# Storing each 512-token output tile with one DMA in place of four, and the last tile in two halves on two queues

## Chip, cores and metric

The kernel runs on one core of one Trainium2 chip. The metric is device time in microseconds (us), the span from the first to the last instruction of an execution. Before the change it took 617.64 us, the median of three runs (613.49 to 619.96). A profiled execution is one run of its own, so its span differs by a few us from the median.

## The reference

Two layers follow one another on `x[8, 3072, 256]` (float32). The first is a frequency mixer along the sequence, the second a gated channel mixer:

```python
def _attn_ref(x, w_r, w_i, b_r, b_i):
    X = np.fft.rfft(x, axis=1)
    Xr, Xi = X.real, X.imag
    Yr = Xr @ w_r - Xi @ w_i + b_r
    Yi = Xr @ w_i + Xi @ w_r + b_i
    # soft threshold of Yr and Yi by 0.01
    return np.fft.irfft(Yr + 1j * Yi, n=x.shape[1], axis=1)

def _moe_ref(x, mu_k, mu_r, w_k, w_v, w_r):
    x_prev = ...                       # x, one token later
    xk = mu_k * x + (1.0 - mu_k) * x_prev
    xr = mu_r * x + (1.0 - mu_r) * x_prev
    k = np.maximum(xk @ w_k, 0.0)      # 256 -> 1024
    v = k * k @ w_v                    # 1024 -> 256
    return 1.0 / (1.0 + np.exp(-(xr @ w_r))) * v
```

## The kernel before

The engines have names in the profiles: PE is the matrix engine, whose results the kernel puts into PSUM (its tile `banks`); DVE and ACT are VectorE and ScalarE. The Fourier transform of 3072 points is split into 96 x 32. Between its two inverse steps the data must change their order, and this goes through device memory: the tile `V` is stored to `Vdr` and read back into `V2`. All these DMAs are issued from the sync queue (`nc.sync`), as the output stores are. Lines are numbered as in the profiles (L465, L476, L523 and so on).

```python
            def store(k):                                   # six of these per batch
                for cj in range(4):
                    nc.sync.dma_start(                                          # L465
                        out=Vdr[b][24 * cj + 4 * u:24 * cj + 4 * u + 4].rearrange("g n d -> n g d"),
                        in_=vt[32 * cj:32 * cj + 32])
                # ... after the sixth of them
            def fetch(k):
                for q in (2, 3, 0, 1):
                    nc.sync.dma_start(out=V2[b, q], in_=Vdr[b][:, 8 * q:8 * q + 8, :])   # L476
# ... cut ...
            # last inverse step: eight such units per batch
            for i in range(4):
                n2 = 16 * half + 4 * i + qd
                for c in range(NCD):
                    nc.tensor.matmul(pv[:, c, :, i, :],                         # L523
                                     V2[b, n2 // 8][:, n2 % 8, 128 * c:128 * c + 128], FI, ...)
```

The last step of the second layer multiplies `v` by the gate and stores 512 tokens. The tile `o` has 128 partitions of 4096 bytes. A tile holds half of each 32 tokens of a third of a batch: partition 32x + s of it has the four neighbouring tokens from number 32s + 16 half + 4x of that third on. So 32 neighbouring partitions go to places 32,768 bytes apart in device memory, and partitions 32 apart go to places 4096 bytes apart:

```python
    def v_unit(t, p):                       # p = 0, 1: two halves of the matmuls
        def issue(ps, h, end):
            # ... 32 matmuls, L653 ...
            if p == 0:
                return
            o, rg = o_pool.tile([128, 4, D], FP32, name="o"), RG[t]      # o_pool has two buffers

            def gated(k):
                nc.vector.tensor_tensor(out=o.rearrange("p q d -> p (q d)"), in0=ps, in1=rg, op=ALU.mult)  # L660
                # ...
            def store(k):
                b, half, hh = t // 6, (t % 6) // 3, t % 3
                rows = out[b].rearrange("(h s z x q) d -> h z x s q d", h=3, s=32, z=2, x=4)
                for xx in range(4):
                    nc.sync.dma_start(out=rows[hh, half, xx], in_=o[32 * xx:32 * xx + 32])   # L669
```

## Time and profile before

| profile of the kernel before | value |
|---|---|
| span | 615.4 us |
| matrix engine busy | 571.8 us, 93% |
| its waits for the V round trip (L523) | 12.6 us |
| its idle time between first and last matmul | 34.5 us |
| last matmul to landing of the last store | 4.85 us |

The matrix engine bounds the kernel. Whatever makes it wait can be expected to cost time. These lines of its page are the clock row (a digit for each fortieth of the span), a group of instructions (busy us, mean ns of one, then the idle time before them and what ended it), and a DMA issue (KB each, median us from issue to landing):

```profile
PEclk9999799999999999989999999999999999999999
...
L523 PE MATMUL banks<-FI,V 96*128 96x96 f16 x512 | 33.5, 216 | 12.9 <-DMA V<-Vdr 12.6
...
out_dram<-o SPq DMA_DIRECT2D x192, 128.0 KB, 2.3
```

The sync queue's own waits (us in total, times, longest):

```profile
SPq L476 <- DMA Vdr<-V: 15.7, 7, 6.2
```

The sync queue waits 15.7 us until V stores have landed, and an output store of 128 KB lands 2.3 us after its issue.

### The profile page before, as it was taken

The numbers are of one execution on the slowest core, as the hardware profiler recorded it, in microseconds if no ns is written. First come the engines' busy times: TensorE is split into PE (matmuls) and PEld (weight loads), VectorE is DVE, ScalarE is ACT, GpSimd is POOL, SyncE is SP. The second block draws the span as 40 slices with busy tenths as digits, with TensorE's granted clock in tenths as the row PEclk, the third lists the DMA queues.
The fourth block names the chain that finished last, engine by engine and source line by source line (L and its number), as shares of the span: only waits on it lengthen the run. The fifth ranks groups of instructions, "written<-read, shape, count | busy, mean of one in ns | idle before, by whom it ended". The sixth has DMA issues, their size and how long they took to land.

```text
span 615.4 us, 12311 instructions
## 1 busy us (share of the span) xinstructions
PE 571.8 (93%) x4823; PEld 431.9 (70%) x4891; DVE 517.6 (84%) x839; ACT 436.0 (71%) x476; POOL 23.3 (4%) x52
## 2 busy tenths in 40 slices
PE   4775899999999999979999999999999999999995
PEld 3764666667777777657776778677776778777664
DVE  6774699878998999959988888979888889989883
ACT  6764596776877677757787768876787777667662
POOL 7001000000000000000000000000000000000000
PEclk9999799999999999989999999999999999999999
DMA  8948237982668755695568946686347833462223
GB/s 150 175 82 181 65 62 166 242 185 55 133 142 236 172 110 132 144 231 118 108 136 200 195 114 129 141 236 147 83 98 189 190 93 87 87 172 65 70 64 78
DMA packets 68686, 84.06 MB, mean 137 GB/s; under 512 B 8978, under 2 KB 53780, under 8 KB 68628
## 3 DMA queue, kind: packets, MB, share of 16 engines
q1 hardware_dynamic: 62916, 69.24, 45.4%
q0 software_dynamic: 5712, 14.03, 14.7%
q8 instruction: 38, 0.62, 0.4%
q14 instruction: 20, 0.16, 0.1%
HBM read 50.07 MB, written 47.19 MB: 158 GB/s over the span
## 4 chain that ended last, share of the span: by engine, by line
PE 79%; DMA 8%; DVE 5%; ACT 5%; issue 2%; SPq 1%; POOL 0%; ACTq 0%; POOLq 0%; DVEq 0%
PE banks L653 25%; PE banks L609 24%; PE banks L426 11%; PE banks L636 6%; DMA V<-Vdr 4%; DMA Vdr<-V 3%; PE banks L523 3%; PE banks L398 3%; PE banks L452 3%; PE banks L280 3%; ACT rl L615 2%; DMA xs<-in_x_dram 1%; DVE Y L442 1%; DVE z L440 1%; DVE V L229 1%
## 5 line engine op out<-in xcount | busy, mean ns | idle before, releaser
L615 ACT ACTIVATE rl<-banks 128x1024 bf16<-128x1024 f32 x192 | 195.4, 1033 | 76.1 <-PE banks L609 75.0
L609 PE MATMUL banks<-xk,wk 128*128 128x512 bf16 x700 | 190.1, 379 | 5.1 <-ACT A L227 0.8
L653 PE MATMUL banks<-wv,k 128*128 128x256 bf16 x1536 | 183.4, 273 | 0.3 <-DVE k L621 0.3
L653 PEld LDWEIGHTS <-k 128*128 128x128 bf16 x1536 | 149.6, 98 | 30.3 <-issue 1.2
L621 DVE TENSOR_TENSOR k<-rl 128x1024 bf16<-128x1024 bf16 x192 | 131.0, 685 | 16.8 <-ACT rl L615 16.1
L609 PEld LDWEIGHTS <-wk 128*128 128x128 bf16 x768 | 73.0, 97 | 59.5 <-issue 3.2
L426 PEld LDWEIGHTS <-XT 128*128 128x128 bf16 x768 | 74.4, 98 | 16.1 <-issue 0.6
L426 PE MATMUL banks<-wr,XT 128*128 128x256 bf16 x384 | 73.5, 273 | 0.2 <-ACT XT L227 0.2
L426 PE MATMUL banks<-wi,XT 128*128 128x256 bf16 x384 | 73.5, 273 | 0.0
L587 DVE SCALAR_TENSOR_TENSOR xk<-diff,muk,YT 128x512 bf16<-128x512 bf16 x96 | 70.0, 745 | 0.5
L587 DVE SCALAR_TENSOR_TENSOR xr<-diff,mur,YT 128x512 bf16<-128x512 bf16 x96 | 68.9, 745 | 0.0
L227 ACT ACTIVATE YT<-banks 128x768 bf16<-128x768 f32 x60 | 46.3, 814 | 30.0 <-PE banks L523 28.1
L660 DVE TENSOR_TENSOR o<-banks,rg 128x1024 f32<-128x1024 f32 x48 | 58.5, 1219 | 6.6 <-PE banks L653 6.6
L227 ACT ACTIVATE z<-banks 128x1024 bf16<-128x1024 f32 x39 | 39.9, 1024 | 23.7 <-PE banks L426 23.7
L227 ACT ACTIVATE XT<-banks 128x1024 bf16<-128x1024 f32 (+2 forms) x45 | 44.4, 989 | 14.3 <-PE banks L398 14.3
L636 PE MATMUL banks<-wrm,xr 128*128 128x256 bf16 x384 | 50.6, 275 | 1.8 <-ACT rl L615 1.7
L641 ACT ACTIVATE rg<-banks 128x1024 bf16<-128x1024 f32 x48 | 49.5, 1031 | 0.9 <-PE banks L636 0.9
L227 ACT ACTIVATE A<-banks 96x1024 bf16<-96x1024 f32 (+1 forms) x43 | 43.4, 1015 | 8.0 <-PE banks L280 6.7
L636 PEld LDWEIGHTS <-xr 128*128 128x128 bf16 x384 | 37.4, 98 | 12.7 <-issue 2.6
L523 PE MATMUL banks<-FI,V 96*128 96x96 f16 x512 | 33.5, 216 | 12.9 <-DMA V<-Vdr 12.6
L227 ACT ACTIVATE V<-banks 128x1024 bf16<-128x1024 f32 x35 | 36.0, 1028 | 13.2 <-PE banks L452 11.1
L523 PEld LDWEIGHTS <-V 96*128 96x128 bf16 x512 | 29.5, 104 | 20.6 <-DMA V<-Vdr 14.7
(98 smaller groups left out, 447.3 us busy)
## 6 DMA issues: line engine op xcount, KB each, us to landing
out_dram<-o SPq DMA_DIRECT2D x192, 128.0 KB, 2.3
xs<-in_x_dram POOLq DMA_DIRECT2D x32, 384.0 KB, 6.2
Vdr<-V SPq DMA_DIRECT2D x192, 64.0 KB, 1.8
V<-Vdr SPq DMA_DIRECT2D x32, 384.0 KB, 6.8
Adr<-A SPq DMA_DIRECT2D x24, 384.0 KB, 5.5
A<-Adr SPq DMA_DIRECT2D x48, 192.0 KB, 5.6
wk<-in_moe_w_k_dram POOLq DMA_DIRECT2D x1, 512.0 KB, 11.6
wv<-in_moe_w_v_dram POOLq DMA_DIRECT2D x1, 512.0 KB, 13.9
```

The costliest lines, as they stand in the source:

```text
L227: nc.scalar.activation(out, in_, AF.Copy, bias=0.0, scale=1.0)
L280: nc.tensor.matmul(ps[:96, 512 * i:512 * i + 512], FT, xt[:, 4 * p + 2 * i:4 * p + 2 * i + 2, :], start=True, stop=True)
L426: nc.tensor.matmul(o, lhs, w[:, c, :], start=(w is wr and c == 0), stop=(w is wi and c == NCD - 1))
L523: nc.tensor.matmul(pv[:, c, :, i, :], V2[b, n2 // 8][:, n2 % 8, 128 * c:128 * c + 128], FI, start=True, stop=True)
L587: nc.vector.scalar_tensor_tensor(out=m[:, c, :], in0=df[:, c, :], scalar=mu[:, c:c + 1], in1=yp[:, c, :], op0=ALU.mult, op1=ALU.add)
L609: nc.tensor.matmul(ps[:, 512 * f:512 * f + 512], wk[:, c, 128 * ff:128 * ff + 128], xk[:, c, :], start=(c == 0), stop=(c == NCD - 1))
L615: nc.scalar.activation(rl, ps, AF.Relu, bias=0.0, scale=1.0)
L621: nc.vector.tensor_tensor(out=k2, in0=rl, in1=rl, op=ALU.mult)
L636: nc.tensor.matmul(ps[:, 256 * q:256 * q + 256], xr[:, c, 128 * q:128 * q + 128], wrm[:, c, :], start=(c == 0), stop=(c == NCD - 1))
L641: nc.scalar.activation(rg, ps, AF.Sigmoid, bias=0.0, scale=1.0)
L653: nc.tensor.matmul(ps[:, 256 * q:256 * q + 256], K2[t][:, ff, 128 * q:128 * q + 128], wv[:, ff, :], start=(ff == 0), stop=(ff == NCF - 1))
L660: nc.vector.tensor_tensor(out=o.rearrange("p q d -> p (q d)"), in0=ps, in1=rg, op=ALU.mult)
```

## The change

Its intent is to save issues on the sync queue (49 output DMAs for 192) and to shorten the end: the last tile is gated in two halves, and the first half is stored from the sync queue while the second is still being computed; the second goes out on the ScalarE queue.

```diff
-            if p == 0:
+            final = t == NT - 1
+            if p == 0 and not final:
                 return
-            o, rg = o_pool.tile([128, 4, D], FP32, name="o"), RG[t]
+            if p == 0 or not final:
+                OT[t] = o_pool.tile([128, 4 * D], FP32, name="o")
+            o, rg = OT[t], RG[t]
+            lo, hi = (512 * p, 512 * p + 512) if final else (0, 1024)
 
             def gated(k):
-                nc.vector.tensor_tensor(out=o.rearrange("p q d -> p (q d)"), in0=ps, in1=rg, op=ALU.mult)
+                nc.vector.tensor_tensor(out=o[:, lo:hi], in0=ps[:, lo:hi], in1=rg[:, lo:hi], op=ALU.mult)
# ... cut ...
             def store(k):
                 b, half, hh = t // 6, (t % 6) // 3, t % 3
-                rows = out[b].rearrange("(h s z x q) d -> h z x s q d", h=3, s=32, z=2, x=4)
-                for xx in range(4):
-                    nc.sync.dma_start(out=rows[hh, half, xx], in_=o[32 * xx:32 * xx + 32])
+                rows = out[b].rearrange("(h s z x q) d -> h z x s (q d)", h=3, s=32, z=2, x=4)[hh, half]
+                (nc.scalar if final and p == 1 else nc.sync).dma_start(out=rows[:, :, lo:hi], in_=o[:, lo:hi])
# ... cut ...
```

The old store writes `[32, 1024]` from 32 partitions, the new one `[4, 32, 1024]` from 128 partitions.

More of the change, by code (lines that the diff above doesn't have):

```diff
@@ L654, in issue @@
                                      wv[:, ff, :], start=(ff == 0), stop=(ff == NCF - 1))
-            if p == 0:
+            final = t == NT - 1
+            if p == 0 and not final:
                 return
-            o, rg = o_pool.tile([128, 4, D], FP32, name="o"), RG[t]
+            if p == 0 or not final:
+                OT[t] = o_pool.tile([128, 4 * D], FP32, name="o")
+            o, rg = OT[t], RG[t]
+            lo, hi = (512 * p, 512 * p + 512) if final else (0, 1024)
             def gated(k):
-                nc.vector.tensor_tensor(out=o.rearrange("p q d -> p (q d)"), in0=ps, in1=rg, op=ALU.mult)
-                e = run_on("dve", k, 1.22)
-                release(h, e)
+                nc.vector.tensor_tensor(out=o[:, lo:hi], in0=ps[:, lo:hi], in1=rg[:, lo:hi], op=ALU.mult)
+                e = run_on("dve", k, 0.7 if final else 1.22)
+                if p == 1:
+                    release(h, e)
                 at(e, store)
@@ L666, in store @@
                 b, half, hh = t // 6, (t % 6) // 3, t % 3
-                rows = out[b].rearrange("(h s z x q) d -> h z x s q d", h=3, s=32, z=2, x=4)
-                for xx in range(4):
-                    nc.sync.dma_start(out=rows[hh, half, xx], in_=o[32 * xx:32 * xx + 32])
+                rows = out[b].rearrange("(h s z x q) d -> h z x s (q d)", h=3, s=32, z=2, x=4)[hh, half]
+                (nc.scalar if final and p == 1 else nc.sync).dma_start(out=rows[:, :, lo:hi], in_=o[:, lo:hi])
+            if p == 0:
+                at(end, gated)
+                return
             done["v_out", t] = end
```

## The prediction

It calls k the number of DMA engines that share one store. For the old store it reads 16 from the starts of packets; 4 for the new one was an assumption of mine, which no trace of the kernel before could show.

> **What bounds the kernel now.** I read the page's busy table and chain first, then the matrix engine's waits, the DMA issues, the sync queue's timeline round the end of one batch, and last the DMA load of single stretches. The page of the kernel before:
>
> ```profile
> span 615.4 us, 12311 instructions
> PE 571.8 (93%) x4823; PEld 431.9 (70%) x4891; DVE 517.6 (84%) x839; ACT 436.0 (71%) x476; POOL 23.3 (4%) x52
> ...
> PE 79%; DMA 8%; DVE 5%; ACT 5%; issue 2%; SPq 1%; POOL 0%; ACTq 0%; POOLq 0%; DVEq 0%
> ```
>
> The matrix engine is busy for 93% of the span and is 79% of the chain that ended last. Its order is fixed when the program is built, so a stall of it is lost. The second owner of the chain is DMA with 8%. The waits of the matrix engine (total us, times, longest) say which DMA:
>
> ```profile
> PE banks L523 <- DMA V<-Vdr: 12.6, 8, 6.3
> PE banks L452 <- DVE Y L442: 5.3, 4, 1.8
> ```
>
> V<-Vdr is a round trip: the tile V is stored to device memory in another order and read back at each batch's end. Output stores appear in no wait of the matrix engine. The sync queue issues all of these; near the end of batch 4 (counted from 0; columns: start, duration, engine, line, what), and the matmuls that need the loads:
>
> ```profile
> 323.55 1.91 SPq L669 DMA_DIRECT2D out_dram<-o  x4
> 325.57 1.84 SPq L465 DMA_DIRECT2D Vdr<-V  x4
> 328.52 0.31 SPq L291 DMA_DIRECT2D Adr<-A  x1
> 329.06 3.03 SPq L476 DMA_DIRECT2D V<-Vdr  x4
> 332.14 2.54 SPq L669 DMA_DIRECT2D out_dram<-o  x4
> 335.92 0.31 SPq L291 DMA_DIRECT2D Adr<-A  x1
> ...
> 338.58 0.51 PE L523 MATMUL banks<-FI,V 96*128 96x96 f16 x8
> ```
>
> An output store is issued just ahead of the batch's last V store, and the second of the V loads, which L523 needs, lands at 337.5, so there is 1.1 us of slack. In batch 3 there is none; its chain of waits holds
>
> ```profile
> 252.06 6.97 DMA Vdr<-V
> ...
> 260.47 8.20 DMA V<-Vdr
> ```
>
> Comparing landing of V loads with the first L523 in every batch, I find slack of about 7 us in batch 1, 0 to 1 in batch 2, 0 in batch 3, 0 to 1 in batch 4, 1.5 in batch 5, 3.5 in batch 6 and 0 in batch 7. Batch 0 has no output stores beside it.
>
> [...] Each old store has 32 rows on both sides[...] its packets start 16 at a time (16 starts from 590.62 to 590.82). The new store is 4 x 32 x 1024 outside and 128 x 1024 inside[...]. No DMA of the kernel before has that shape[...]. [...] The trace's fastest 4096-byte packets take 158 ns, 25.9 GB/s[...].[...]
>
> **The change part by part.**
>
> *Issues.* 192 stores become 47 whole ones and 2 halves, so 143 issues fewer. The median issue takes 0.42 us, so the sync queue is freed of 60 us. It is no bound: 1% of the chain. What that saves on the path is the time by which a V store stands behind the four issues: at 325.57 where the copy of V ended at 325.10, so 0.4 us, and 1.3 us in batch 7 (535.58 against 534.28).
>
> *Engines of a store.* 512 KB is 128 packets of 4096 bytes. On 4 engines each moves 32: 32 x 0.158 = 5.1 us; with 0.8 us from issue to first packet and about 0.5 from last packet to landing, a store lands some 6.4 us after its issue. Now, four issues take 1.7 us and the last lands 2.2 us after its own, so 3.5 us after the first one starts.
>
> *Load of these four engines.* All stores make 48 x 5.1 = 243 us for each. The two large queues take 60.1% of 16 engines' 615 us, 5,920 engine-us; stores are 6,144 packets of about 0.28 us (the tail's median), 1,720; the rest is 4,200, or 262 us per engine. So four engines would be busy for 505 us (82%), the twelve others for 43%. No saturation[...].
>
> *The V store behind an output store.* In batch 4 the store is issued at 323.55 and keeps four engines until 323.55 + 0.8 + 5.1 = 329.45. Their part of the four V stores is 32 packets of 512 bytes at 27 to 44 ns, about 1 us, and 0.8 to landing: 331.2, against 328.75 now. So the loads slip by 2.5 us. The same sum gives about 2 in batches 2, 5 and 7, and I take 3 for batch 3, where an input load shares the engines. Less the slack: 1.5 + 3 + 2.3 + 1 + 0 + 1.8 = 9.6 us of new stalls.
>
> *The A round trip.* Adr<-A at 335.92 stands behind the V loads and the next output store. The stretch is one of full load (columns of the windows view as on the page; DMA share and GB/s are last):
>
> ```profile
> 328.50:345.10 16.60, 16.24 (x144) 12.01 (x144) 13.24 (x24) 12.38 (x14) 0.51 (x1) 1.00 0.88 223
> ```
>
> With 48 packets per engine for the rest instead of 56 and 32 more for the stores on the four, I get 48 x 0.295 + 5.1 = 19.3 us instead of 16.5. The readers of A have 2 to 6 us of slack and the matrix engine is itself late by then, so I count 2 us for the two batches with the least.
>
> *The tail.* Tiles end every 7.8 us there:
>
> ```profile
> 597.60:605.40 7.80, 7.75 (x57) 5.44 (x57) 3.99 (x6) 4.78 (x6) 0.00 (x0) 1.00 0.29 69
> ...
> 609.58 1.22 DVE o L660
> ```
>
> The last gate ends at 610.80, its fourth store lands at 614.34. Halving the gate ends the second half at about 609.58 + 0.65 = 610.2, and the first lies beside the matmuls. But both halves are again on the same four engines, behind the previous tile's store (issued at 605.06, packets from 605.9 to 611.0). The halves add 2 x 2.7 = 5.4 us: 616.4, and 616.9 landed. So the tail gets 2.5 us longer where the intent was about 2 us shorter.
>
> Sum: 9.6 + 2 + 2.5 = 14 us over 617.6, about 632 us.
>
> **The rivals.** *All 16 engines take part after all*[...]. Then only the issue time and the halved tail remain: 1.3 + 0.4 + about 1.8 saved, 614 us, so within 2%. *The four engines are slow but hidden*: [...]the slack of batches 1, 5 and 6 swallows it; the tail alone remains, 620 us. The fact that stores appear in no wait of the matrix engine speaks for it; the zero slack in batches 3 and 7 against it. *The four engines become a bound*: if their packets take 0.25 us or more under mixed load (the median of all 4096-byte packets is 0.252), stores alone take 390 us and the four come near full; every round trip then slips by 5 us or more, and the time goes to 645 us or above.
>
> **Range and chances.** k = 4 I hold for 88% likely. Under it 620 to 648 with the middle at 632, which lies just above the 2% line of 630; without it 612 to 617. Runs of the kernel before spread from 613.5 to 620.0, which blurs the line further. A range of 618 to 648 holds it 8 times in 10. Faster by over 2%: 0.02; within 2%: 0.43; slower: 0.55.
>
> **What would show it.** Packets of an output store start 4 at a time; its landing takes 6 to 7 us instead of 2.3 in the issue list; the wait of L523 for V<-Vdr grows from 12.6 us to above 20; the sync queue waits longer for Vdr<-V (15.7 us now); the last store lands 6 us or more after the last gate instead of 3.5. Landing in 2 to 4 us would refute k = 4. Long landings with an unchanged L523 wait would refute the step from engines to stalls. A long wait of the gate for its output buffer would mean that I overlooked the two buffers of o.

## The result

The changed kernel took 665.64 us (median of four runs, 663.6 to 667.4) against 617.41 us for the kernel before on the same chip (median of four, the three runs above among them). The ratio is 1.0786, with a 95% interval of 1.0721 to 1.0851. A ratio here is the mean time of one kernel's fast runs over that of the other's of the same rounds, so it is not quite the ratio of the medians. A second session gave 665.42 us and 1.0794. The change costs 48 us, and the forecast of 632 us, with its range of 618 to 648, was too low.

The head of the page of the changed kernel, with its chain that ended last:

```profile
span 661.5 us, 12122 instructions
PE 588.5 (89%) x4823; PEld 440.5 (67%) x4891; DVE 518.7 (78%) x840; ACT 437.5 (66%) x476; POOL 23.1 (3%) x52
...
PEclk9987899999997999889997999979999899979997
...
PE 71%; DMA 14%; DVE 7%; ACT 3%; issue 2%; SPq 1%; POOL 1%; ACTq 0%; POOLq 0%; DVEq 0%
```

Two things changed at once. DMA has gone from 8% to 14% of the chain. The matrix engine does the same 4823 recorded matmuls, yet is busy for 16.7 us more (588.5 against 571.8). The clock row says why: there is now a dip at the end of nearly every batch, and the mean granted clock is 0.952 instead of 0.987.

The waits of the engines, those of the sync queue, and the group of L523:

```profile
PE banks L523 <- DMA V<-Vdr: 34.5, 23, 3.9
DVE o L664 <- DMA out_dram<-o: 6.2, 3, 2.6
```

```profile
SPq L476 <- DMA Vdr<-V: 39.9, 11, 6.2
...
SPq L465 <- DMA out_dram<-o: 8.9, 6, 2.3
```

```profile
L523 PE MATMUL banks<-FI,V 96*128 96x96 f16 x512 | 39.7, 234 | 34.7 <-DMA V<-Vdr 34.5
```

The wait for the V round trip grew from 12.6 to 34.5 us, and the sync queue's wait for the V stores from 15.7 to 39.9. Two waits are new: the gate waits for its output buffer, and the V stores stand behind an output store. A mean L523 matmul went from 216 to 234 ns, because 201 of the 512, and not 75, now start at half clock. By the clock records one takes 206 ns at full clock and 278 to 279 at half, in both kernels.

One batch shows the mechanism. This is the sync queue at the end of batch 4 (start, duration, engine, line, what), to be laid beside the same stretch of the kernel before in the prediction:

```profile
336.14 0.54 SPq L673 DMA_DIRECT2D out_dram<-o  x1
337.72 5.45 SPq L465 DMA_DIRECT2D Vdr<-V  x4
343.26 0.37 SPq L291 DMA_DIRECT2D Adr<-A  x1
350.15 2.39 SPq L476 DMA_DIRECT2D V<-Vdr  x4
```

The output store is issued once, at 336.14, and now takes 0.54 us instead of four issues in 1.91. But the four V stores behind it take 5.45 us to issue instead of 1.84, and the loads follow 7.0 us after the last of these, at 350.15, where the kernel before had 1.65 us between the two. In the semaphore records of the trace the output store lands at 347.29, and the V stores at 348.0 to 350.1. The records show which updates are late; I take each for the report of one engine. The output store's four come at 344.2, 344.4, 346.1 and 347.3. Of the 16 of the first V store 12 have come by 340.1, and the other four follow at 344.4, 344.6, 347.5 and 348.0, each 0.2 to 1.4 us after one of the output store's. The matrix engine starts L523 when the first load lands, at 354.7, and is then in this state (windows view: length, busy time and count of PE, PEld, DVE, ACT, POOL, then granted clock, DMA share, GB/s):

```profile
355.00:362.00 7.00, 5.13 (x33) 3.04 (x32) 1.64 (x7) 3.35 (x4) 0.00 (x0) 0.58 0.66 205
362.00:369.00 7.00, 6.95 (x64) 5.18 (x63) 3.84 (x6) 4.49 (x5) 0.00 (x0) 0.93 0.60 132
```

The granted clock is 0.58 in the first of them. It had been 1.00 up to the stall.

The six batches from 2 to 7, from the issue of the first of the last four V stores, in us:

| batch | before: stores landed | before: first L523 | after: stores landed | after: first L523 |
|---|---|---|---|---|
| 2 | 3.2 | 12.6 | 12.0 | 16.8 |
| 3 | 8.4 | 12.6 | 12.0 | 16.4 |
| 4 | 3.2 | 13.0 | 12.4 | 17.0 |
| 5 | 3.9 | 13.2 | 12.5 | 16.4 |
| 6 | 3.2 | 13.2 | 9.9 | 13.8 |
| 7 | 3.3 | 10.0 | 10.1 | 14.4 |

The stores land 7.3 us later in the mean. Some of that is given back, most likely because the loads then find emptier engines (in batch 4 the DMA share is 0.88 from 350.20 to 355.00, where it was 0.99 from 329.00 to 337.50 before the change). The first L523 comes 3.3 us later in the mean, 20 us over six batches, which is nearly the 21.9 us that its wait grew by.

The end of the changed kernel, from the timeline:

```profile
645.07 4.05 SPq L673 DMA_DIRECT2D out_dram<-o  x2
...
649.54 0.69 DVE L664 TENSOR_TENSOR o<-banks,rg 128x512 f32<-128x512 f32 x1 [0.98 <-PE banks L653]
650.26 1.15 ACTq L673 DMA_DIRECT2D out_dram<-o  x1
```

The gate does end earlier relative to the matmuls, at 650.2 with the last matmul at 649.5. But the two halves land at 660.45 and 660.14. Last matmul to last landing takes 11.0 us instead of 4.85.

So the 46.1 us between the two profiles are, in sum, 23.1 us more idle time of the matrix engine between its first and last matmul (21.9 of them at L523), 6.3 us at the two ends (nearly all in the tail), and 16.7 us of longer busy time. Whether this last part is a cost of its own was tested below.

One trap of the page: its list of issues has no landing time for the changed store.

```profile
out_dram<-o SPq DMA_DIRECT2D x47, 512.0 KB
```

The page infers the landing from 16 semaphore updates for a DMA. Here the counts match only if an output store gives five: four late ones and one at once. The store issued at 645.07 has one 0.96 us after its issue and four at 8.16, 8.25, 10.54 and 10.59; the last old store in the trace before has 16, from 1.83 to 2.21 us after its issue. That each late update stands for one engine in use is my reading. A missing number in this list was the quickest sign that the store no longer ran on 16 engines. (The V and A transfers, which share its semaphores, lose their numbers too, so it is a sign and no proof.) With five updates a store, the median landing is 10.9 us, the least 8.9.

### The profile page after: what moved, and what is told of

It reads as the page before. It is cut to its first block, busy times and chain, and to the rows that moved or that the text cites. A ratio compares the mean times of both kernels' runs of the same rounds, so it can differ in the third digit from the quotient of the medians.

```text
span 661.5 us, 12122 instructions
## 1 busy us (share of the span) xinstructions
PE 588.5 (89%) x4823; PEld 440.5 (67%) x4891; DVE 518.7 (78%) x840; ACT 437.5 (66%) x476; POOL 23.1 (3%) x52
## 4 chain that ended last, share of the span: by engine, by line
PE 71%; DMA 14%; DVE 7%; ACT 3%; issue 2%; SPq 1%; POOL 1%; ACTq 0%; POOLq 0%; DVEq 0%
PE banks L653 22%; PE banks L609 21%; PE banks L426 10%; DMA V<-Vdr 7%; PE banks L636 6%; DMA out_dram<-o 4%; PE banks L523 3%; PE banks L452 3%; PE banks L398 3%; PE banks L280 2%; DMA Vdr<-V 2%; DVE k L621 1%; DVE o L664 1%; ACT V L227 1%; DVE Y L442 1%
## 5 line engine op out<-in xcount | busy, mean ns | idle before, releaser
L609 PE MATMUL banks<-xk,wk 128*128 128x512 bf16 x700 | 195.0, 386 | 5.7 <-issue 0.9
L609 PEld LDWEIGHTS <-wk 128*128 128x128 bf16 x768 | 74.2, 99 | 61.2 <-issue 6.5
L523 PE MATMUL banks<-FI,V 96*128 96x96 f16 x512 | 39.7, 234 | 34.7 <-DMA V<-Vdr 34.5
L664 DVE TENSOR_TENSOR o<-banks,rg 128x1024 f32<-128x1024 f32 (+1 forms) x49 | 58.6, 1197 | 10.9 <-DMA out_dram<-o 6.2
L523 PEld LDWEIGHTS <-V 96*128 96x128 bf16 x512 | 33.0, 114 | 48.5 <-DMA V<-Vdr 42.7
L227 ACT ACTIVATE z<-banks 128x1024 bf16<-128x1024 f32 x39 | 39.9, 1024 | 23.7 <-PE banks L426 23.7
L636 PE MATMUL banks<-wrm,xr 128*128 128x256 bf16 x384 | 54.1, 288 | 0.6 <-ACT rl L615 0.2
L636 PEld LDWEIGHTS <-xr 128*128 128x128 bf16 x384 | 39.0, 103 | 12.5 <-issue 1.0
L227 ACT ACTIVATE V<-banks 128x1024 bf16<-128x1024 f32 x35 | 36.0, 1027 | 13.2 <-PE banks L452 10.0
```

Source lines behind the costliest of these rows:

```text
L227: nc.scalar.activation(out, in_, AF.Copy, bias=0.0, scale=1.0)
L523: nc.tensor.matmul(pv[:, c, :, i, :], V2[b, n2 // 8][:, n2 % 8, 128 * c:128 * c + 128], FI, start=True, stop=True)
L609: nc.tensor.matmul(ps[:, 512 * f:512 * f + 512], wk[:, c, 128 * ff:128 * ff + 128], xk[:, c, :], start=(c == 0), stop=(c == NCD - 1))
L636: nc.tensor.matmul(ps[:, 256 * q:256 * q + 256], xr[:, c, 128 * q:128 * q + 128], wrm[:, c, :], start=(c == 0), stop=(c == NCD - 1))
L664: nc.vector.tensor_tensor(out=o[:, lo:hi], in0=ps[:, lo:hi], in1=rg[:, lo:hi], op=ALU.mult)
```

## The experiments

All 15 runs gave correct results. Each quotes the kernel before of its own session, whose medians were 616.59 to 617.73 us. They test four questions: which part of the change costs the time, whether it is the number of engines of a store (theory A) or something else that comes with one large store (rival B) or its place in the queue (F), whether engines that read partitions 32 apart hinder each other (theory P, against N for no hindrance), and whether the half clock is a cost of its own (C against W; `k4_warm` calls C theory H). In the expectations of `one_whole` and `four_split`, rival C is something else: the split tail. All runs but `four_split`, the `k4_warm` runs, `after_again` and the other two named `_split` leave the split tail out.

| run | what it is | us | ratio to before (95%) |
|---|---|---|---|
| one_whole | the change without the split tail | 663.18 | 1.0746 (1.0683 to 1.0809) |
| four_split | before, with the split tail alone | 617.85 | 1.0025 (0.9978 to 1.0072) |
| turn_k16 | one DMA per tile, 16 engines, by turned matmul output | 628.33 | 1.0167 (1.0134 to 1.0199) |
| turn_four_k4 | four DMAs of 32 partitions, 4 engines each | 645.30 | 1.0444 (1.0420 to 1.0469) |
| turn_two_k4 | two DMAs of 64 partitions, 4 engines each | 662.57 | 1.0748 (1.0696 to 1.0801) |
| k4_act | one_whole with all output stores on the ScalarE queue | 696.39 | 1.1287 (1.1234 to 1.1341) |
| k4_warm | the change, with 20 idle matmuls in each stall | 657.41 | 1.0662 (1.0594 to 1.0729) |
| k4_warm2 | the same with 6 to 18 idle matmuls | 660.59 | 1.0720 (1.0657 to 1.0782) |
| after_again | the change again | 665.42 | 1.0794 (1.0747 to 1.0841) |
| k4_warm_again | k4_warm again, same session as after_again | 658.51 | 1.0671 (1.0626 to 1.0717) |
| evac_k16_split | 16 engines, turned in the copy, split tail | 636.80 | 1.0321 (1.0282 to 1.0360) |
| half_k16 | the same with another tile layout, no split | 611.63 | 0.9940 (0.9897 to 0.9983) |
| half_k16_split | half_k16 with the split tail | 610.21 | 0.9920 (0.9872 to 0.9968) |
| half_four_k8 | half layout, four DMAs on 8 engines each | 628.07 | 1.0191 (1.0116 to 1.0266) |
| half_two_k16 | half layout, two DMAs on 16 engines | 611.09 | 0.9914 (0.9861 to 0.9966) |

### Which part of the change: one_whole and four_split

`one_whole` takes the split tail away:

```diff
-            final = t == NT - 1
+            final = False
```

> The changed kernel without the split of the last tile: all 48 tiles by one DMA of 4 x 32 x 1024. Theory A (the number of DMA engines): 662 to 668 us, the wait of the FI,V matmuls for V<-Vdr near 34 us, half-clock episodes after each batch as in the changed kernel. Rival C (the split tail is to blame): under 650 us.

It took 663.18 us, as theory A has it, and its wait at L523 is 34.1 us, as in the changed kernel. `four_split` leaves the four stores of 32 rows and has only the split tail:

```diff
-                (nc.scalar if final and p == 1 else nc.sync).dma_start(out=rows[:, :, lo:hi], in_=o[:, lo:hi])
+                for xx in range(4):
+                    (nc.scalar if final and p == 1 else nc.sync).dma_start(
+                        out=rows[xx, :, lo:hi], in_=o[32 * xx:32 * xx + 32, lo:hi])
```

> The kernel before with only the last tile gated and stored in two parts on two queues, each part by four DMAs of 32 rows (16 engines). Theory A: 1 to 2 us faster than before, from last gate to end shorter. Rival C: slower than before by 5 us or more.

It took 617.85 us, no measurable difference. In its profile the time from the last matmul to the last landing falls from 4.85 to 3.94 us. The 0.9 us is there, but is smaller than the interval of the timed runs. Joining the four DMAs into one thus costs some 45 us (663.18 against 617.73), and splitting the tail costs and gains next to nothing.

### One DMA on 16 engines: turn_k16

If the cost lies in the four engines, one DMA of the same 512 KB on 16 of them should not have it. The old stores have 32 rows outermost on both sides and give 16 updates each, so the new one is to have 32 outermost on both sides too, and the partitions must lie in the order (s, x) instead of (x, s). `turn_k16` lets the L523 matmuls write their results in that order, and the later tiles follow it:

```diff
-                    YT[b] = yt_pool.tile([128, NCD, 3, 2, 20, 32], BF16, name="YT")
+                    YT[b] = yt_pool.tile([128, NCD, 3, 2, 5, 32, 4, 1], BF16, name="YT")
-                    "p c (h n s) -> p c h n s", h=3, n=4)
+                    "p c (h a n e) -> p c n (h a) e", h=3, n=4, a=32, e=1)
# ... the copies of the margin and the readers of YT follow ...
-                rows = out[b].rearrange("(h s z x q) d -> h z x s (q d)", h=3, s=32, z=2, x=4)[hh, half]
+                rows = out[b].rearrange("(h s z x q) d -> h z s x (q d)", h=3, s=32, z=2, x=4)[hh, half]
```

> Columns within a group of 128 tokens are reordered from (x, s) to (s, x) where the matmuls of the last transform write PSUM, so that one DMA of 32 x 4 x 1024 stores the tile; no split.[...] Theory A: 612 to 622 us, each store lands within 4.5 us where nothing competes, wait of the FI,V matmuls for V<-Vdr 8 to 16 us. Rival B (one large DMA in place of four small ones is to blame, through its issue or its semaphore): 650 us or more.

At 628.33 us it missed the forecast of theory A (612 to 622), and lies far below that of the rival, for which the size of one DMA was to blame. The group of L523 shows why it missed:

```profile
L523 PE MATMUL banks<-FI,V 96*128 96x96 f16 x512 | 53.9, 296 | 9.6 <-DMA V<-Vdr 9.6
```

The wait for V is 9.6 us, less than before the change, and the stores land 3.0 us after their issue at the end. But each of these matmuls takes 296 ns instead of 216, in all 20 us more, because it now writes its 96 results 16 bytes apart. I had not taken this into account. By the clock records one takes 282 ns at full clock, and 206 in the kernel before. Not every pattern with gaps does this: the kernel before writes three runs of 128 bytes, `turn_four_k4` below runs of 32 bytes, `half_k16` one run, and all three take 206 ns at full clock.

### How many engines, and which partitions they read: turn_four_k4, turn_two_k4

Both keep four engines per DMA, but cut the tile into four or two DMAs. With the columns in the order (a, x, b), a = 4 or 2, each DMA writes 4 x 8 x 1024 from 32 partitions, or 4 x 16 x 1024 from 64:

```diff
-                rows = out[b].rearrange("(h s z x q) d -> h z x s (q d)", h=3, s=32, z=2, x=4)[hh, half]
-                (nc.scalar if final and p == 1 else nc.sync).dma_start(out=rows[:, :, lo:hi], in_=o[:, lo:hi])
+                rows = out[b].rearrange("(h a b z x q) d -> h z a x b (q d)", h=3, a=4, b=8, z=2, x=4)[hh, half]
+                for j in range(4):
+                    (nc.scalar if final and p == 1 else nc.sync).dma_start(
+                        out=rows[j, :, :, lo:hi], in_=o[32 * j:32 * j + 32, lo:hi])
```

> Four DMAs per tile again, 32 partitions each, but columns ordered (a, x, b) with a = 4 and b = 8, so that each DMA is 4 x 8 x 1024 and runs on 4 engines. Theory A: 655 to 672 us, as the changed kernel. Rival B (one DMA instead of four): 612 to 622 us.

> Two DMAs per tile of 64 partitions each, 4 x 16 x 1024, so again 4 engines each and 32 packets of 4096 bytes per engine and tile; columns ordered (a, x, b) with a = 2. Theory P ([...]the pattern of partitions sets the rate per packet): in the tail the last store of a tile lands 9.5 to 11 us after the first issue, as with one DMA (10.1), and 655 to 668 us. Rival N (the rate rises with the number of DMAs, since four DMAs of 4 engines landed about 7 us after the first issue): 8 to 8.8 us, and 648 to 656 us.

`turn_four_k4` took 645.3 us: neither theory. Four engines with four small DMAs cost 28 us over the kernel before, but 18 us less than four engines with one. Its stores of the last tile were issued from 636.26 on and landed at 639.62, 640.86, 642.14 and 643.39. The last is 7.1 us after the first issue, and the pieces come 1.25 us apart, which is 8 packets at 0.156 us on each engine. In the changed kernel the first store of the tail (issued at 598.91, with no other transfer beside it) took 10.07 us. Its four engines reported 8.08, 8.19, 9.88 and 10.07 us after the issue. The packet records don't name the engine, but they fall into four rows of packets that follow each other almost without gaps, and I take these for the engines. In two rows 32 packets take 6.6 to 6.7 us, in the others 8.4 to 8.5 (0.21 and 0.26 us each). In `turn_four_k4` they take 5.4 to 5.5 us (0.17 each). What stands before the first packet and after the last is alike: 1.2 to 1.3 and 0.2 to 0.4 us. Two thirds of the packets of the slow store still take 159 ns; the others take up to 0.75.

If each engine takes one index of the outermost dimension (an assumption, as the records don't name the engine), the difference between the two stores is the rows that an engine reads while the others work: 8 partitions apart in the one, 32 apart in the other. That 32 is the distance which hinders was a conjecture of mine. `turn_two_k4` tests it: on the same assumption its four engines read 16 partitions each, so the first and third are 32 apart. Theory P forecast 655 to 668 us, and 662.57 came. The last landing is 9.9 us after the first issue, as P had it (9.5 to 11), and not the 8 to 8.8 of its rival. Halving the size of each DMA thus bought nothing, and the time of `one_whole` came back.

The distance alone doesn't make a packet slow. In the last tile of `one_whole` each engine reports 5.3 to 5.5 us after it has reported the store before (656.57 to 658.62 after 651.12 to 653.12), which is 0.17 us per packet with partitions 32 apart (on the same assumption). There two of the engines are some 1.8 us behind the other two, so at any time they should read other rows. This fits a hindrance that acts only while two engines read rows 32 apart at the same time, but no run tested it.

### The place in the queue: k4_act

Another thought was that the harm comes from standing ahead of the V stores in one queue. Then the ScalarE queue should take it away:

```diff
-                (nc.scalar if final and p == 1 else nc.sync).dma_start(out=rows[:, :, lo:hi], in_=o[:, lo:hi])
+                nc.scalar.dma_start(out=rows[:, :, lo:hi], in_=o[:, lo:hi])
```

> All 48 stores by one DMA of 4 x 32 x 1024, issued on the scalar engine's queue instead of the sync queue that carries V. Theory A (the four engines themselves are occupied, whichever queue feeds them): 645 to 670 us, waits for V<-Vdr of 25 us or more. Rival F (only the order within the sync queue holds V's packets back): 615 to 635 us, waits for V<-Vdr under 16 us.

It took 696.39 us, the slowest of all, outside the ranges of both theories. The waits of the matrix engine:

```profile
PE banks L523 <- DMA V<-Vdr: 54.0, 18, 8.4
```

A second queue didn't spare the V round trip, it did the reverse. In the sync queue the next output store is issued behind the V loads; from the other queue it is issued as soon as the gate ends, and now runs beside them (in batch 4 at 359.51, with the V loads issued at 363.47). The median landing of a V load went from 6.6 us in the changed kernel to 8.9.

### The half clock: k4_warm, k4_warm2, k4_warm_again

In the changed kernel the clock records give half rate for 6.8 us after the stall of each of batches 2 to 7. Apart from the one at the end, which lasts 10.7 us, the half-rate records of its trace last 3.4, 6.8 or 10.2 us. How long a wait has to be was not tested: the longest waits at L523 in batches 5 and 6 were 2.8 and 1.7 us, and half clock followed. `k4_warm` fills each stall with matmuls whose result nobody reads:

```diff
+                if n == 0 and b >= 2:
+                    for _ in range(20):
+                        nc.tensor.matmul(ps[:, 0:512], ident, G.rearrange("p g c j k -> p (g c j k)")[:, 0:512],
+                                         start=True, stop=True)
                 for i in range(4):
```

> The changed kernel with 20 idle matmuls of 128 x 512 into the bank that the first FI,V matmuls of batches 2 to 7 overwrite afterwards, so that TensorE is busy while it would wait for V<-Vdr. Theory H (the stalls drop the granted clock to one half for some 6.8 us each, and this makes up 17 of the 48 us): the half-clock episodes of these batches go, 644 to 656 us. Rival (the lower clock has another source, or costs nothing): 662 to 670 us.

It took 657.41 us, just above the forecast of 644 to 656. The half clock after the stalls was gone but for one stretch of 3.4 us, but 20 idle matmuls take 4.5 us, more than the stalls, and ended up to 3.9 us after the load had landed. `k4_warm2` took fewer, 17, 16, 18, 13, 6 and 13:

> As k4_warm with 17, 16, 18, 13, 6 and 13 idle matmuls in batches 2 to 7, since the 20 ended up to 3.9 us after the loads had landed (8.6 us in all). Theory H: 646 to 655 us with half-clock episodes in at most two of these batches. Rival (k4_warm's gain of about 8 us is all that the clock is worth): 656 to 662 us.

This missed: 660.59 us. Two half-clock stretches were back (6.8 us at 205, 3.4 us at 362), and the wait for V had grown from 12.6 to 21.8 us. Sized so closely, idle matmuls don't hold. The time lies in the rival's range (656 to 662), but with half clock back it doesn't settle what the clock is worth. As both runs belonged to sessions without the changed kernel, the two were repeated side by side with five rounds:

> The changed kernel again, only so that the next run can be compared with it in the same session. Both theories: 661 to 668 us, half-clock stretches of about 6.8 us after the stall of each of batches 2 to 7.

> The changed kernel with idle matmuls in the stalls, as in k4_warm. Theory C (the half-clock stretches after the stalls are a term of their own, about 8 us net of the idle matmuls' overshoot): 655 to 660 us, at least 5 us under the changed kernel of the same session. Rival W (the slower clock only lengthens work that then waits for the same transfers anyway): within 3 us of the changed kernel of the same session.

The changed kernel took 665.42 us, the one with idle matmuls 658.51, 6.9 us less. This is theory C. The clock row of `k4_warm_again` and two of its groups, the real V matmuls (now L527) and the idle ones (L522):

```profile
PEclk9998899999999999999999999999999999999997
```

```profile
L527 PE MATMUL banks<-FI,V 96*128 96x96 f16 x512 | 33.7, 214 | 18.8 <-DMA V<-Vdr 18.5 <-ACT YT L227 0.2
...
L522 PE MATMUL banks<-G,ident 128*128 128x512 f16 x120 | 26.9, 379 | 0.0
```

The V matmuls are back at 214 ns. Without the idle ones the matrix engine is busy for 601.4 - 26.9 = 574.5 us, 18.7 less than in `after_again` (593.2). (The profile of the changed kernel quoted above lacks the records of 68 L609 matmuls which these two have, so its 588.5 can't be compared with them.) Of these 18.7 us 6.9 became time. The idle matmuls took 26.9 us where the first waits of the six batches had been 17.3, so 9.6 us went to them. Another 3.5 are a longer first wait in batch 0, where nothing had been changed. So at least some 6.9 of the 48 us are the clock's own; that nearly all of the longer busy time is lost time is likely, but not shown.

### A version without the cost: evac_k16_split, half_k16, half_k16_split

To have 16 engines without the slower matmuls, the L523 matmuls may write contiguously, and the copy out of PSUM read with a stride:

```diff
-                    "p c (h n s) -> p c h n s", h=3, n=4)
+                    "p c (n r) -> p c n r", n=4)
# ...
-                                 "p c (h r) -> p c h r", h=3), 0.8, 0.95)
+                                 "p c (n h s) -> p c h s n", h=3, n=4), 0.8, 0.95)
```

> One DMA of 32 x 4 x 1024 per tile over 16 engines, split last tile; the reordering of columns is done by the copy out of PSUM (its read is strided), so the FI,V matmuls write contiguous rows. Theory A: the FI,V matmuls return from 296 to about 210 ns, and the time is 603 to 614 us, below the kernel before. Rival (the single DMA of 16 engines has a cost of its own beside the strided write): 618 us or more.

At 636.8 us this missed by over 20 us. The L523 matmuls were back at 211 ns, but two new waits had come up:

```profile
ACT YT L227 <- DVE xr L590: 26.7, 7, 4.1
...
PE banks L639 <- ACT YT L227: 16.6, 6, 2.8
```

The copy into `YT` waited for a reader of `YT` that reads the other half of it. My reading is that the program takes the copy's write, which now steps through more dimensions, for one range from its first to its last byte. This range overlaps the other half, and so the two are put in order. (`turn_k16` has the same tile and no such wait; its copy writes whole runs.) How the program tests for overlap was not looked at; the next run tests the remedy. Making the half the outermost dimension takes the two ranges apart:

```diff
-                    YT[b] = yt_pool.tile([128, NCD, 3, 2, 5, 32, 4, 1], BF16, name="YT")
+                    YT[b] = yt_pool.tile([128, 2, NCD, 3, 5, 32, 4], BF16, name="YT")
```

> One DMA of 32 x 4 x 1024 over 16 engines per tile, no split; the copy out of PSUM reorders the columns, and the tile YT keeps the two halves apart, so that its writes can't be taken to overlap reads of the other half. Theory A: the wait of the copy to YT for the reader xr (26.7 us in evac_k16_split) goes, FI,V matmuls at about 215 ns, and 604 to 613 us, below the kernel before. Rival (the single DMA of 16 engines costs something itself): 617 us or more.

> As half_k16, with the last tile gated and stored in two parts on two queues. Theory A: 603 to 613 us, 0 to 1.5 us below half_k16. Rival (the split costs a later end): above half_k16 by 1 us or more.

`half_k16` took 611.63 us, and 610.21 with the split tail. The latter is the best median of all, 0.8% under the kernel before, but the two are not told apart by their runs. The wait of the copy is gone, and the copies into `YT` on ACT take no longer for their stride (46.6 us in all, for 46.3 before). The copies of the margin on DVE take 13.7 us for 9.3. The clock row of `half_k16_split`, its group of L523 and its output stores:

```profile
PEclk9997699999999999999999999999999999999999
```

```profile
L523 PE MATMUL banks<-FI,V 96*128 96x96 f16 x512 | 32.7, 214 | 6.1 <-DMA V<-Vdr 5.8 <-ACT YT L227 0.2
```

```profile
out_dram<-o SPq DMA_DIRECT2D x47, 512.0 KB, 3.3
...
out_dram<-o ACTq DMA_DIRECT2D x1, 256.0 KB, 2.5
```

The wait for V is 5.8 us against 12.6 in the kernel before: this is about what the intent of the change is worth when the store keeps its 16 engines (the new layout is in it too). From the last matmul to the last landing it takes 3.25 us instead of 4.85. The list of issues also prints landing times again.

### The dose between: half_four_k8 and half_two_k16

Two more runs use the half layout. `half_four_k8` stores each tile by four DMAs of 8 x 4 x 1024, and `half_two_k16` by two of 16 x 4 x 1024:

```diff
-                (nc.scalar if final and p == 1 else nc.sync).dma_start(out=rows[:, :, lo:hi], in_=o[:, lo:hi])
+                for j in range(4):                                    # half_two_k16: 2
+                    (nc.scalar if final and p == 1 else nc.sync).dma_start(
+                        out=rows[8 * j:8 * j + 8, :, lo:hi],          # 16 * j:16 * j + 16
+                        in_=o[32 * j:32 * j + 32, lo:hi])             # 64 * j:64 * j + 64
```

By the count of packets under 512 bytes (given in the next section) they ran on 8 and on 16 engines. That the packets would be quick again on 8, as theory P has it, was an estimate of mine that no trace had shown.

> The same order of columns as half_k16, but four DMAs of 32 partitions, 8 x 4 x 1024[...]. Theory P[...]: each store lands within 1.9 to 2.3 us in the tail, as the old stores of 16 engines did, and 606 to 620 us. Rival N (each engine needs 0.27 to 0.33 us per packet[...]): 2.5 to 2.9 us in the tail, and above 620 us.

> As half_k16, but each tile is stored by two DMAs of 64 partitions (16 x 4 x 1024) on 16 engines. Theory P ([...]its packets take about 0.32 us): from first issue to last landing of the last tile 3.7 to 4.0 us, 612 to 622 us in time. Rival N ([...]packets stay at 0.16 to 0.17 us): 3.1 us or less, 608 to 614 us.

In `half_four_k8` the stores of the last tile landed 2.33 to 2.38 us after their issue, just above the forecast of P, but the time of 628.07 us lies above its range. The sync queue of batch 4:

```profile
323.74 3.11 SPq L674 DMA_DIRECT2D out_dram<-o  x4
326.97 1.95 SPq L465 DMA_DIRECT2D Vdr<-V  x4
```

Four issues took 3.11 us, where the kernel before needed 1.91 for its four. So the V stores came later; the last of them met an input load that started at 327.94, and landed at 333.2. The wait at L523 was 15.9 us, against 7.4 in `half_k16`. In this batch the issue time that the change wanted to save delayed a V store; how much of the 16 us over `half_k16` it makes up was not tested. The four runs lie between 622.74 and 631.93, so against the kernel before the verdict at 2% is unclear.

`half_two_k16` took 611.09 us, with 3.59 us from first issue to last landing: between the forecasts (3.7 to 4.0 for P, 3.1 or less for N), with a time that fits N. The packets are of both kinds: the first 64 of the last tile have a median of 267 ns, the last 64 one of 159. Why only the first 64 are slow was not shown. At 16 engines, whatever slows them matters too little to be seen in the time. In `half_k16`, where one DMA reads all 128 partitions on 16 engines, no packet of the last tile takes over 175 ns.

## Why the prediction was wrong

*The bound and the victim: right.* The matrix engine bounds the kernel, the V round trip is where it waits, and the stores reach it only through the V stores. L523's wait did grow above 20 us (34.5), the sync queue's wait for V stores did grow, and the last store did land more than 6 us after the gate.

*Four engines: right.* I had assumed 4, and the trace has four late updates for each store. The packets under 512 bytes fell, before and after:

```profile
DMA packets 68686, 84.06 MB, mean 137 GB/s; under 512 B 8978, under 2 KB 53780, under 8 KB 68628
```

```profile
DMA packets 65936, 84.03 MB, mean 127 GB/s; under 512 B 6102, under 2 KB 50904, under 8 KB 65880
```

The difference of 2876 is 192 x 16 - 49 x 4: beside the 5906 that don't belong to output stores, 16 of these packets for each store before and 4 after, one for each late update. In the same way, the other runs that store all tiles alike have 16 for each store where its outermost dimension is 32 (`turn_k16` and `half_k16`, 6674 in all) or 16 (`half_two_k16`, 7442), 8 where it is 8 (`half_four_k8`, 7442), and 4 where it is 4 (`one_whole` and `k4_act`, 6098; `turn_two_k4`, 6290; `turn_four_k4`, 6674). `turn_k16` and `half_k16` undo it: the wait at L523 is 9.6 and 7.4 us there, and in `half_k16` the whole cost is gone.

*Issue time: right in size, but not all of it.* An output store's issue takes 0.54 us instead of four times 0.42. That V stores behind it would take 5.45 us to issue, in place of 1.84, was not foreseen; single V stores take up to 2.9 us.

*Landing of a store in "some 6.4 us": this step failed.* A store with nothing beside it took 10.07 us, and the median of the changed kernel was 10.9. The term of the sum that was mis-sized is the 32 x 0.158 = 5.1 us for the packets of one engine: they took 6.6 to 6.7 us on two engines and 8.4 to 8.5 on the other two, so 0.21 and 0.26 us per packet. The fixed parts, 0.8 + 0.5, were nearly right (1.2 + 0.3). I had taken the fastest packet of the trace for all of them. It is the most frequent even now (159 ns), but a third of the packets take longer, up to 0.75 us. The trace before held the warning: its store packets at the end took 0.28 us in the median, and I had put that to 16 engines working at once. That alone doesn't do it: in `half_k16`, where 16 engines work at once too, no packet of the last tile takes over 175 ns. In `turn_four_k4` 0.17 us was measured.

*V stores behind the output store: the same error, carried on.* In batch 4 they were to land 7.7 us after the output store's issue, and landed after 14.0. The forecast of 9.6 us of stalls became 21.9. The third rival, "the four engines become a bound", had named the threshold of 0.25 us per packet and a time of 645 or above for it. With 0.26 us on the slower engines and 665 us it came close (the first L523 slipped by 3.3 us, not the 5 that it named), and deserved more than the tail of the range.

*Two slips in the working.* For batch 5 the sum has 1 us where 2 less 1.5 is 0.5. And the first L523 matmuls need the first V load, not the second: in the changed kernel four of them run at 354.71, as the first load lands (354.67), and the next wait for the second (356.32). Neither matters beside the rest.

*The A round trip: right.* One wait of 2.0 us (L381, for A from its copy in memory), where 2 had been counted.

*The tail: right in sign, too small.* 6.3 us instead of 2.5, again by the packets' rate and the queue: the two halves stand behind a store that itself lands only at 655.65.

*A term that was missing: the clock.* I counted a stall of 4 us as 4 us. In the trace of the changed kernel half clock for 6.8 us follows each such stall. The busy time grew by 16.7 us, and at least 6.9 us of this are time lost, by `k4_warm_again`. In the trace before, the stall of batch 3 (2.5 us at 263.6) was followed by a half-clock stretch of 3.4 us at 268.5, which would have told me.

Together: 21.9 + 2.0 + 6.3 in place of 9.6 + 2 + 2.5, and 16.7 of slower clock in place of none, 46.9 us against the 46.1 between the two profiles.

*Left open.* What slows the packets of some stores isn't settled: `turn_two_k4` fits theory P, `half_two_k16` half of it. How much of the 16.7 us of slower clock is lost time could not be shown beyond 6.9. What the gate's new wait for its buffer (6.2 us) costs on the path was not tested with a third buffer. A store on four engines whose packets all take 0.17 us was run only in four pieces, not in one.

## What to carry to other kernels

Before joining DMAs, write down the access pattern of the joined one as the instruction carries it, and look at its outermost dimension: here 143 fewer issues cost 48 us, because each store fell from 16 engines to 4 (32 outermost before, 4 after), and it was the V stores behind it that paid, landing 7.3 us later. If the layout stands against it, turn the data where this is free (in a copy that has to be made anyway), not in the matmul's output (611.63 us in `half_k16`, 628.33 in `turn_k16`). And where a change adds stalls to the matrix engine, even of 2 or 3 us, look for a slower clock after them too (here 6.8 us at half clock in batches whose longest waits were 1.7 and 2.8 us).
